# An attention kernel whose ring for x keeps six batches instead of eight

## The chip, the cores and the metric

One core of a Trainium2 chip. The metric is the device time of one execution in microseconds (us); lower is better. "A" and "B" are the two halves of the problem, and a "unit" is one head of one batch (512 units, 256 in A and then 256 in B). The kernel works the units off in order.

## The reference, cut to what matters

Two equal attention blocks with their own inputs, whose outputs are put side by side (16 batches, 144 rows of width 448, 16 heads of 256, 512 cached keys, all bfloat16):

```
q = (x @ wq).reshape(B, Sq, H, Dh).transpose(0, 2, 1, 3)
scores = einsum("bhqd,bhkd->bhqk", q, k_cache) * Dh ** -0.5
o = einsum("bhqk,bhkd->bhqd", softmax(scores), v_cache)
out = o.transpose(0, 2, 1, 3).reshape(B, Sq, H * Dh) @ wo
```

## The kernel before

A scheduler of the kernel's own writes one instruction list per engine, in the order of a loop over units, and puts in only the waits that are needed. Step `i` of the loop issues the Q product of unit `i+3`, the scores of unit `i+2`, and the product with V, the softmax sum and some output projection of unit `i`. All loads are issued by one queue (SP) in one fixed order.

First, x arrives transposed in groups of four batches, in a ring of eight:

```
LQ, LS, LT = 3, 2, 4
KW, KR = 16, 32
NV, NXG = 9, 2
XB = 4
# ... cut ...
xt_sb = sb("xt_sb", [128, 4, NXG * XB * SQ], BF16)
# ... cut ...
def t_load_x(XG):
    pr, j = divmod(XG, Bn // XB)
    sl = XG % NXG
    c0 = sl * XB * SQ
    x = xs[pr][j * XB:(j + 1) * XB].rearrange("b q d -> (b q) d")
    def e(q):
        q.dma_start_transpose(xt_sb[:, 0:3, c0:c0 + XB * SQ], x[:, 0:384]).then_inc(sems["xt%d" % sl], 16)
        return q.dma_start_transpose(xt_sb[:, 3, c0:c0 + XB * SQ], x[:, 320:448]).then_inc(sems["xt%d" % sl], 16)
    # ... cut ...
```

Second, Q is computed for two neighbouring batches of one head at once (8 matmuls of 288 columns) where the two lie side by side in the ring; where they don't, one batch at a time (8 matmuls of 144 columns each). For odd heads that happens at batches 7 and 8:

```
def q_pair(U):          # how many batches the Q product at unit U computes
    b, h = unit(U)[1:]
    # ... cut: single products in the first four batches of A ...
    if h % 2 == 0:
        return 2 if b % 2 == 0 else 0
    j = b % (NXG * XB)
    return 1 if j in (0, NXG * XB - 1) else (2 if j % 2 else 0)
```

Third, K arrives transposed, one load of 4.19 MB for 16 units ("K step" n serves units 16n to 16n+15), with V in between, and where A gives way to B the query weights (q0 to q3) and the output weights (o0 to o7) of B have to be loaded too. The order there is fixed by hand:

```
MID = ("k16 v127 v128 q0 v129 v130 q1 v131 q2 q3 v132 k17 v133 v134 v135 v136 v137 o0 o1 v138 o2 v139 o3 v140 o4 v141 "
       "o5 v142 o6 o7 k18")
# ... cut: each x load goes into the order just ahead of the first K load that may come after it
elif fn is t_load_k:
    lo = KW * (args[0] + 1) - KR - LS               # earliest step: the K slot is free
elif fn is t_load_x and args[0] >= NXG:
    lo = (args[0] - NXG + 1) * XB * H - LQ          # earliest step: the x slot is free
elif fn is t_load_wq and args[0]:
    lo = NU - H + 4 * args[1] + 4 - LQ              # earliest step: A is done with these weights
```

## Time and profile before

| | |
|---|---|
| time, median of 4 | 1066.06 us (1065.64 to 1066.65) |
| the profiled execution | 1063.18 us, span 1061.4 us |
| PE (TensorE) busy | 98% |
| share of PE in the chain that ended last | 97% |
| PE idle for loads, in all | 12.7 us |

The page of the profile gives the busy time of each engine, the queues by which DMA packets were moved, and the chain of work that ended last (the share of the span that lies with each engine or line). PE is TensorE, PEld its weight loads, DVE VectorE, ACT ScalarE, POOL GpSimd; SPq is the queue of loads, and L1018 is line 1018 of the kernel.

```profile
PE 1043.1 (98%) x12736; PEld 895.5 (84%) x12736; DVE 670.9 (63%) x2063; ACT 706.4 (67%) x2133; POOL 625.6 (59%) x1030
...
q8 instruction: 102, 1.67, 0.6%
...
PE 97%; DMA 2%; SPq 1%; DVE 0%; issue 0%; ACT 0%; DVEq 0%
PE s_ps L1052 24%; PE ot_ps L1097 24%; PE qp_ps L1018 24%; PE op_ps L1196 20%; PE ot_ps L1109 3%; DMA v_sb<-in_A_k_cache_dram 1%; PE s_ps L972 1%; PE qp_ps L972 1%; PE qp_ps L1196 1%; DMA v_sb<-in_B_v_cache_dram 1%; SPq L922 0%; SPq L923 0%; DVE ost_sb L1217 0%; SPq L902 0%; DVE run_sb L1154 0%
```

PE is busy nearly throughout and is nearly the whole chain. "q8 instruction" is, as its count will show, the queue that fetches PE's program: 102 packets of 16 KB.

The view of waits lists what PE waited for (total us, number of waits, longest):

```profile
PE s_ps L972 <- DMA v_sb<-in_A_k_cache_dram: 6.1, 4, 4.7
PE qp_ps L1018 <- DMA xt_sb<-in_A_x_dram: 3.6, 1, 3.6
PE ot_ps L1097 <- DMA v_sb<-in_B_v_cache_dram: 3.0, 1, 3.0
```

(The first three K steps are an exception to the transposed loads: their K comes in plain tiles of 512 KB into the buffers of V, hence `v_sb<-in_A_k_cache`, and PE transposes them.) So PE waits for K, x and V only 12.7 us in all. The first load of x is at fault for 3.6 us near the start. The queue's own timeline (start, duration, what) shows why: the two transposes of the first x load hold the queue 3.57 and 1.87 us, and the second K tile cannot be issued before 7.97 us:

```profile
2.44 3.57 SPq L922 DMA_TRANSPOSE xt_sb<-in_A_x_dram  x1
6.05 1.87 SPq L923 DMA_TRANSPOSE xt_sb<-in_A_x_dram  x1
7.97 0.59 SPq L953 DMA_DIRECT2D v_sb<-in_A_k_cache_dram  x1
```

In the chain of waits, start and duration of a Q product of two batches (0.98 us) and of one batch (0.50 us):

```profile
555.67 0.98 PE qp_ps L1018 x8
558.09 0.50 PE qp_ps L1018 x8
```

Two single products cost 1.00 us and a pair 0.98: PE is paid by columns, not by instructions.

PE's timeline between the problems (start, duration, what, in brackets the idle time before and its cause):

```profile
566.88 1.14 PE L1097 MATMUL ot_ps<-pt_sb,v_sb 128*128 128x144 bf16 x8 [3.05 <-DMA v_sb<-in_B_v_cache_dram]
...
568.68 2.13 PE L1018 MATMUL qp_ps<-xt_sb,wq_sb 128*128 128x288 bf16 x8
...
573.04 0.66 PE L1018 MATMUL qp_ps<-xt_sb,wq_sb 128*128 128x144 bf16 x8
```

V comes 3.05 us late, and for some 6 us after it matmuls run at half speed: the 8 matmuls of the pair at 568.68 take 2.13 us, where 1.14 is usual in this view.

### The profile page before, as it was taken

The numbers are of one execution on the slowest core, as the hardware profiler recorded it, in microseconds if no ns is written. First come the engines' busy times: TensorE is split into PE (matmuls) and PEld (weight loads), VectorE is DVE, ScalarE is ACT, GpSimd is POOL, SyncE is SP. The second block draws the span as 40 slices with busy tenths as digits, with TensorE's granted clock in tenths as the row PEclk, the third lists the DMA queues.
The fourth block names the chain that finished last, engine by engine and source line by source line (L and its number), as shares of the span: only waits on it lengthen the run. The fifth ranks groups of instructions, "written<-read, shape, count | busy, mean of one in ns | idle before, by whom it ended". The sixth has DMA issues, their size and how long they took to land.

```text
span 1061.4 us, 32383 instructions
## 1 busy us (share of the span) xinstructions
PE 1043.1 (98%) x12736; PEld 895.5 (84%) x12736; DVE 670.9 (63%) x2063; ACT 706.4 (67%) x2133; POOL 625.6 (59%) x1030
## 2 busy tenths in 40 slices
PE   6999999999999999999998999999999999999997
PEld 6999888888888888888887888888888888888885
DVE  4776666666666666666665666666666666666664
ACT  4887656667756666666855666676775666667674
POOL 3554555656656566666754656566665555666663
PEclk9999999999999999999998999999999999999999
DMA  9999999999999999999999999999999999999950
GB/s 304 379 350 285 295 293 254 274 297 273 292 276 298 208 280 267 290 292 298 262 287 352 265 274 290 291 290 301 264 263 265 304 285 289 289 290 279 239 187 13
DMA packets 588801, 294.15 MB, mean 277 GB/s; under 512 B 500576, under 2 KB 513376, under 8 KB 588640
## 3 DMA queue, kind: packets, MB, share of 16 engines
q1 hardware_dynamic: 588640, 291.99, 109.1%
q8 instruction: 102, 1.67, 0.6%
q14 instruction: 59, 0.48, 0.2%
HBM read 161.48 MB, written 4.13 MB: 156 GB/s over the span
## 4 chain that ended last, share of the span: by engine, by line
PE 97%; DMA 2%; SPq 1%; DVE 0%; issue 0%; ACT 0%; DVEq 0%
PE s_ps L1052 24%; PE ot_ps L1097 24%; PE qp_ps L1018 24%; PE op_ps L1196 20%; PE ot_ps L1109 3%; DMA v_sb<-in_A_k_cache_dram 1%; PE s_ps L972 1%; PE qp_ps L972 1%; PE qp_ps L1196 1%; DMA v_sb<-in_B_v_cache_dram 1%; SPq L922 0%; SPq L923 0%; DVE ost_sb L1217 0%; SPq L902 0%; DVE run_sb L1154 0%
## 5 line engine op out<-in xcount | busy, mean ns | idle before, releaser
L1072 POOL TENSOR_TENSOR pp_sb<-pt_sb 128x288 f32<-128x288 bf16 x512 | 374.0, 731 | 345.7 <-ACT pt_sb L1062 323.5
L1062 ACT ACTIVATE pt_sb<-s_ps 128x288 bf16<-128x288 f32 x1024 | 364.4, 408 | 268.5 <-PE s_ps L1052 268.0
L1154 DVE TENSOR_REDUCE run_sb<-ot_ps 1x1 bf16<-1x144 f32 x1024 | 262.3, 293 | 324.0 <-ACT rinv_sb L1120 324.0
L1097 PE MATMUL ot_ps<-pt_sb,v_sb 128*128 128x144 bf16 x4096 | 340.7, 226 | 3.0 <-DMA v_sb<-in_B_v_cache_dram 3.0
L1052 PE MATMUL s_ps<-qt_sb,kt_sb 128*128 128x144 bf16 x4096 | 340.8, 226 | 0.0
L1052 PEld LDWEIGHTS s_ps<-qt_sb,kt_sb 128*128 128x128 bf16 x4096 | 288.2, 98 | 43.5 <-DVE qt_sb L1032 0.2
L1018 PE MATMUL qp_ps<-xt_sb,wq_sb 128*128 128x288 bf16 (+1 forms) x2496 | 305.3, 266 | 3.6 <-DMA xt_sb<-in_A_x_dram 3.6
L1076 POOL TENSOR_TENSOR ps_sb<-pp_sb 128x144 bf16<-128x144 f32 x512 | 250.8, 490 | 76.2 <-PE ot_ps L1109 3.1
L1018 PEld LDWEIGHTS qp_ps<-xt_sb,wq_sb 128*128 128x128 bf16 x2496 | 218.8, 98 | 79.0 <-issue 4.4
L1196 PE MATMUL op_ps<-wo_sb,ring 128*128 128x448 bf16 x1120 | 285.0, 353 | 0.4 <-DVE ring L1140 0.4
L1097 PEld LDWEIGHTS ot_ps<-pt_sb,v_sb 128*128 128x128 bf16 x4096 | 274.6, 98 | 3.7 <-DMA v_sb<-in_B_v_cache_dram 3.2
L1140 DVE TENSOR_TENSOR ring<-ot_ps,rinv_sb 128x288 bf16<-128x288 f32 (+2 forms) x640 | 231.0, 375 | 0.0
L1120 ACT ACTIVATE rinv_sb<-ot_ps 128x144 f32<-128x144 f32 x512 | 150.1, 293 | 51.0 <-PE ot_ps L1109 8.0
L1032 DVE CAST qt_sb<-qp_ps 128x576 bf16<-128x576 f32 x200 | 151.1, 755 | 41.7 <-PE qp_ps L1018 37.6
L1125 ACT ACTIVATE rinv_sb<-rinv_sb 128x144 f32<-128x144 f32 x512 | 165.4, 323 | 16.1
L1109 PE MATMUL ot_ps<-ps_sb,ones 128*128 128x144 bf16 x512 | 115.9, 226 | 0.0
L1196 PEld LDWEIGHTS op_ps<-wo_sb,ring 128*128 128x128 bf16 x1120 | 94.0, 98 | 21.8 <-DVE ring L1140 0.8
L1031 DVE CAST qt_sb<-qp_ps 128x288 bf16<-128x288 f32 x112 | 49.2, 439 | 9.4 <-PE qp_ps L1018 8.8
L1109 PEld LDWEIGHTS ot_ps<-ps_sb,ones 128*128 128x128 bf16 x512 | 50.2, 98 | 0.0
L980 ACT ACTIVATE kt_sb<-qp_ps 128x512 bf16<-128x512 bf16 x48 | 28.9, 603 | 8.5 <-PE qp_ps L972 8.5
L972 PE MATMUL s_ps<-qt_sb,v_sb 128*128 128x128 bf16 x192 | 19.4, 226 | 6.2 <-DMA v_sb<-in_A_k_cache_dram 6.1
L980 DVE COPY kt_sb<-s_ps 128x512 bf16<-128x512 bf16 x48 | 19.5, 405 | 6.3 <-PE s_ps L972 6.2
(21 smaller groups left out, 85.1 us busy)
## 6 DMA issues: line engine op xcount, KB each, us to landing
v_sb<-in_A_v_cache_dram SPq DMA_DIRECT2D x128, 512.0 KB, 6.9
v_sb<-in_B_v_cache_dram SPq DMA_DIRECT2D x128, 512.0 KB, 7.1
v_sb<-in_A_k_cache_dram SPq DMA_DIRECT2D x24, 512.0 KB, 9.3
out_dram<-ost_sb SPq DMA_DIRECT2D x36, 112.0 KB, 6.1
wo_sb<-in_A_wo_dram SPq DMA_DIRECT2D x8, 448.0 KB, 8.5
wo_sb<-in_B_wo_dram SPq DMA_DIRECT2D x8, 448.0 KB, 8.9
wq_sb<-in_A_wq_dram SPq DMA_DIRECT2D x4, 768.0 KB, 9.2
wq_sb<-in_B_wq_dram SPq DMA_DIRECT2D x4, 768.0 KB, 10.1
```

The costliest lines, as they stand in the source:

```text
L1018: ins = t.matmul(acc, lhsT=wq_sb[:, kc, c0:c0 + 128], rhs=xt_sb[:, kc, xo:xo + n * SQ], start=(kc == 0), stop=(kc == 3))
L1032: return v.tensor_copy(qt_sb[:, a:b + 1:b - a, :, :], qp_ps[:, :, 0:2 * SQ].rearrange("p e (u q) -> p u e q", u=2))
L1052: ins = t.matmul(s_ps[bank][:, (c % 2) * SQ:(c % 2 + 1) * SQ], lhsT=kt_sb[:, 2 * c + dc, ko:ko + 128], rhs=qt_sb[:, qsl, dc, :], start=(dc ...
L1062: return a.activation(pt_sb[:, psl, 2 * k:2 * k + 2, :].rearrange("p b q -> p (b q)"), s_ps[bank][:, 0:2 * SQ], AF.Exp, scale=DH ** -0.5)
L1072: return g.tensor_tensor(pp_sb[:, :, :], pt_sb[:, psl, 0:2, :], pt_sb[:, psl, 2:4, :], op=ALU.add)
L1076: return g.tensor_tensor(ps_sb[:, sl, :], pp_sb[:, 0, :], pp_sb[:, 1, :], op=ALU.add)
L1097: ins = t.matmul(ot_ps[ob][:, dc * SQ:(dc + 1) * SQ], lhsT=v_sb[:, vsl, j, c * DH + dc * 128:c * DH + (dc + 1) * 128], rhs=pt_sb[:, sl, c, ...
L1109: return t.matmul(ot_ps[ob][:, 2 * SQ:3 * SQ], lhsT=ones[:, :], rhs=ps_sb[:, sl, :], start=True, stop=True)
L1125: return a.activation(rinv_sb[:, sl, :], ln, AF.Exp, scale=-1.0)
L1140: ins = v.tensor_tensor(ring[:, 2 * h:2 * h + 2, r0:r0 + q1 - q0], ot_ps[ob][:, 0:2 * SQ].rearrange("p (c q) -> p c q", c=2)[:, :, q0:q1], ...
L1154: return v.tensor_reduce(run_sb[0:1, k, j:j + 1], ot_ps[ob][0:1, 2 * SQ:3 * SQ], axis=AX.X, op=op)
L1196: ins = t.matmul(acc[0:m, 0:D], lhsT=ring[:, c, col0:col0 + m], rhs=wo_sb[:, c, :], start=(c == first), stop=(c == last))
```

## The change

Its intent: keep x for six batches only, which frees 2.3 KB per partition of SBUF (not used yet), load the first two batches alone so that work starts sooner, and let a pair of batches wrap round the ring, so that the odd heads of batches 7 and 8 are paired as well. The diff, cut to its core:

```diff
-    NV, NXG = 9, 2
+    NV, NX = 9, 6
-    XB = 4
+    X_GROUPS = ((0, 2), (2, 6), (6, 10), (10, 14), (14, 18), (18, 20), (20, 24), (24, 28), (28, 32))
@@ t_load_x
+            cuts = [g for g in range(g0, g1) if g == g0 or g % NX == 0 or g % Bn == 0] + [g1]
+                for a, b in zip(cuts, cuts[1:]):   # one pair of transposes for each piece
@@ q_pair
-            j = b % (NXG * XB)
-            return 1 if j in (0, NXG * XB - 1) else (2 if j % 2 else 0)
+            return 1 if b in (0, Bn - 1) else (2 if b % 2 else 0)
@@ t_q
-                                       rhs=xt_sb[:, kc, xo:xo + n * SQ], start=(kc == 0), stop=(kc == 3))
+                                       rhs=xt_sb[:, kc, xo:xe + 1:max(xe - xo, 1), :], start=(kc == 0), stop=(kc == 3))
@@ earliest step of an x load
+            last = X_GROUPS[XG][1] - NX
+            return last * H - LQ if last > 0 else s_min
```

One consequence is not in the diff: the order of loads changes. Before, x is loaded ahead of K steps 5, 9, 13, 19, 21 and 25. After, it is loaded ahead of 5, 9, 13, 15, 19, 23 and 27. The load ahead of step 15 (batches 2 and 3 of B) is new there.

## The prediction

> What bounds the kernel. TensorE: the page's busy table gives PE 1043.1 of 1061.4 us (98%), clock 0.996; the chain of waits is PE for 97%. The DMA engines are nine tenths busy in nearly every slice, but in the waits view PE idles little for them: 6.1 us for K rows (s_ps L972), 3.6 us for x (qp_ps L1018), 3.0 us for V (ot_ps L1097). In time order: the first Q product waits until 9.96 us for x, the second K row tile is used at 12.39 us, waits of 0.3 and 0.2 us follow at 25.7 and 34.0 us; then PE has no gap until 563.8 us, where V is 3.05 us late behind problem B's second K load (26.85 us in the queue), and for 6 us after it matmuls run at half speed (8 pair matmuls in 1.92 us, not 0.98).
>
> What the change does.
> 1. Q. Odd heads of batches 7 and 8 of both problems join: 32 single products become 16 pairs, 128 matmuls (of 12736) fewer. But PE is paid by columns: in the chain a single product takes 0.50 us, a pair 0.98, so each pairing saves 0.02 us, 0.3 us in all. The Trainium skill ("TensorE: Matmul & The Clock Gate", Back-to-back issue gap) gives N/2.4 + 2.5 ns per warm matmul; 0.50/8 = 62 ns and 0.98/8 = 122 ns agree. DVE trades 32 casts of 439 ns for 16 of 755 ns, off the chain (63% busy).
> 2. Start. The first x load has two batches instead of four. Its two transposes held the queue 3.57 + 1.87 us, so the second K tile was issued only at 7.97 us; this is on the chain (SPq L922, L923, then DMA into v_sb). Halved, I estimate 2.5 us off. Afterwards the DMA engines are saturated (387 GB/s) and PE touches their limit at 25.7 and 34.0 us; both shift together, so the gain should stay.
> 3. Later x loads. 24 transposes instead of 16, same bytes. The second load is now needed at unit 29 (about 78 us); it left the queue at 64.7. Later ones are due 16 or 17 units (32 us) before use, just ahead of a K load. An x plus a K load held the queue 22 to 28 us (K alone 16 to 27). The last two move ahead of the K loads issued at 736 and 863 us; K and V have, I estimate, 3 to 5 us to spare there, as at existing x loads, which stalled nothing.
> 4. The SBUF freed is not used.
>
> Sum: 1066.05 - 2.5 - 0.3, plus 0.3 for the chance of a new stall: 1063.5 us. The gap at 564 us should stay. A new stall would cost its length plus some 3 us of half clock.
>
> Range 1059.5 to 1068. Faster by over 2%: 1%; within 2%: 97%; slower by over 2%: 2%.
>
> What would show it: 12608 PE instructions, yet the Q lines' time on the chain only 0.3 us lower; first Q product at about 7.5 us, second K tile used at about 9.8 us, all later work earlier by that; PE idle on x about 1 us; the gap near 561 us still 3 us.
>
> What would make it wrong: a half-size transpose costs the queue as much as a whole one (gain under 1 us); an x load late at a wrap, or pushing K or V late: PE waiting on xt_sb, kt_sb or v_sb with half-clock work after it (+3 to +8 us each); the 564 us gap closing or growing with DMA timing.

## The result, and the profile after

The changed kernel took 1066.12 us (median of 4, 1065.60 to 1067.24), the kernel before 1066.06. The ratio is 1.0002, 95% interval 0.9984 to 1.0019: the same. (A ratio here is the mean time of one kernel's fast executions over that of the other's of the same rounds, so it is not quite the ratio of the medians.) The time lies in the predicted range, but the gain that was forecast, 2.5 us, is not there.

The page after:

```profile
PE 1044.1 (98%) x12608; PEld 892.0 (84%) x12608; DVE 671.0 (63%) x2047; ACT 706.0 (66%) x2133; POOL 625.6 (59%) x1030
...
q8 instruction: 101, 1.65, 0.6%
...
PE 96%; DMA 3%; SPq 0%; DVE 0%; issue 0%; ACT 0%; DVEq 0%
PE s_ps L1063 24%; PE ot_ps L1108 24%; PE qp_ps L1029 23%; PE op_ps L1207 20%; PE ot_ps L1120 3%; DMA v_sb<-in_A_k_cache_dram 1%; PE s_ps L977 1%; PE qp_ps L977 1%; DMA v_sb<-in_B_v_cache_dram 1%; DMA wq_sb<-in_B_wq_dram 1%; PE qp_ps L1207 1%; DMA xt_sb<-in_A_x_dram 0%; SPq L925 0%; DVE ost_sb L1228 0%; SPq L902 0%
```

PE has 128 matmuls and 128 weight loads fewer, and its program needs one packet of 16 KB fewer (101 instead of 102).

At the start the queue is free 2.8 us earlier, as forecast: the two transposes take 1.43 and 1.23 us, and the second K tile is issued at 5.19 us instead of 7.97:

```profile
2.44 1.43 SPq L925 DMA_TRANSPOSE xt_sb<-in_A_x_dram  x1
3.91 1.23 SPq L926 DMA_TRANSPOSE xt_sb<-in_A_x_dram  x1
5.19 0.58 SPq L958 DMA_DIRECT2D v_sb<-in_A_k_cache_dram  x1
```

The waits of PE are others, though:

```profile
PE s_ps L977 <- DMA v_sb<-in_A_k_cache_dram: 5.8, 3, 4.9
PE qp_ps L1029 <- DMA wq_sb<-in_B_wq_dram: 3.6, 1, 3.6
PE qp_ps L1029 <- DMA xt_sb<-in_A_x_dram: 2.4, 1, 2.4
PE s_ps L1063 <- DMA kt_sb<-in_B_k_cache_dram: 1.9, 1, 1.9
PE ot_ps L1108 <- DMA v_sb<-in_B_v_cache_dram: 1.1, 2, 0.6
```

The wait for x is 1.2 us shorter and the one for V in B 1.9 us, but two are new: 3.6 us for the query weights of B and 1.9 us for K of B. The first of them in PE's timeline:

```profile
534.02 2.08 PE L1029 MATMUL qp_ps<-xt_sb,wq_sb 128*128 128x288 bf16 x8 [3.58 <-DMA wq_sb<-in_B_wq_dram]
535.90 1.17 PE L1063 MATMUL s_ps<-qt_sb,kt_sb 128*128 128x144 bf16 x8
...
539.47 0.66 PE L1063 MATMUL s_ps<-qt_sb,kt_sb 128*128 128x144 bf16 x8
```

The idle time of 3.58 us is followed by half-speed work (2.08 us for the pair at 534.02).

To see where time goes, I read from the timelines the start of one instruction that each unit has exactly once (the logarithm on ScalarE, 512 of them) and took the difference after minus before, unit by unit:

| unit | after minus before, us | what lies between |
|---|---|---|
| 0 | -2.18 | the start |
| 32 to 96 | -1.75 | nothing changes |
| 124 | +2.10 | Q of batch 8 is computed early, with batch 7 |
| 140 to 224 | -1.90 | it is given back in batch 8: net -0.16 |
| 256 | +4.36 | wait for the query weights of B, and half-speed work |
| 267 | -0.97 | before has its V wait here, after only 0.6 us |
| 288 | +3.52 | wait for K step 18, and half-speed work |
| 320 to 352 | +3.38 | nothing changes |
| 416 to 480 | +3.22 | batches 7 and 8 of B: again -0.16 |

So the start gives 1.75 us and each set of pairs 0.16 us, and the lead of 1.90 us is there up to unit 240. It is lost between units 240 and 288. (The 3.2 us at the end is more than the timed executions show: the profiled execution of the kernel before, 1063.18 us, was a fast one.)

The queue's timeline shows what comes ahead of the late weights. Before:

```profile
475.91 16.30 SPq L932 DMA_TRANSPOSE kt_sb<-in_A_k_cache_dram  x1
...
505.82 16.97 SPq L932 DMA_TRANSPOSE kt_sb<-in_B_k_cache_dram  x1
...
523.97 0.47 SPq L900 DMA_DIRECT2D wq_sb<-in_B_wq_dram  x1
```

After:

```profile
471.09 1.22 SPq L925 DMA_TRANSPOSE xt_sb<-in_B_x_dram  x1
...
474.01 19.36 SPq L937 DMA_TRANSPOSE kt_sb<-in_A_k_cache_dram  x1
...
503.92 19.62 SPq L937 DMA_TRANSPOSE kt_sb<-in_B_k_cache_dram  x1
...
524.73 0.47 SPq L900 DMA_DIRECT2D wq_sb<-in_B_wq_dram  x1
```

K step 16 (the transpose at 505.82 before, 503.92 after) holds the queue for 19.62 us instead of 16.97, and the query weights, issued behind it, come that much later in relation to the work. K step 15 (at 474.01) holds it for 19.36 us; before it was 16.30 (at 475.91).

### The profile page after: what moved, and what is told of

It reads as the page before. It is cut to its first block, busy times and chain, and to the rows that moved or that the text cites. A ratio compares the mean times of both kernels' runs of the same rounds, so it can differ in the third digit from the quotient of the medians.

```text
span 1064.6 us, 32119 instructions
## 1 busy us (share of the span) xinstructions
PE 1044.1 (98%) x12608; PEld 892.0 (84%) x12608; DVE 671.0 (63%) x2047; ACT 706.0 (66%) x2133; POOL 625.6 (59%) x1030
## 4 chain that ended last, share of the span: by engine, by line
PE 96%; DMA 3%; SPq 0%; DVE 0%; issue 0%; ACT 0%; DVEq 0%
PE s_ps L1063 24%; PE ot_ps L1108 24%; PE qp_ps L1029 23%; PE op_ps L1207 20%; PE ot_ps L1120 3%; DMA v_sb<-in_A_k_cache_dram 1%; PE s_ps L977 1%; PE qp_ps L977 1%; DMA v_sb<-in_B_v_cache_dram 1%; DMA wq_sb<-in_B_wq_dram 1%; PE qp_ps L1207 1%; DMA xt_sb<-in_A_x_dram 0%; SPq L925 0%; DVE ost_sb L1228 0%; SPq L902 0%
## 5 line engine op out<-in xcount | busy, mean ns | idle before, releaser
L1029 PEld LDWEIGHTS qp_ps<-xt_sb,wq_sb 128*128 128x128 bf16 x2368 | 213.3, 99 | 81.7 <-issue 7.5
L1043 DVE CAST qt_sb<-qp_ps 128x576 bf16<-128x576 f32 x216 | 163.3, 756 | 49.5 <-PE qp_ps L1029 45.4
L1042 DVE CAST qt_sb<-qp_ps 128x288 bf16<-128x288 f32 x80 | 35.2, 440 | 5.7 <-PE qp_ps L1029 5.1
```

The lines of the kernel that those rows point to most:

```text
L1029: ins = t.matmul(acc, lhsT=wq_sb[:, kc, c0:c0 + 128], rhs=xt_sb[:, kc, xo:xe + 1:max(xe - xo, 1), :], start=(kc == 0), stop=(kc == 3))
L1043: return v.tensor_copy(qt_sb[:, a:b + 1:b - a, :, :], qp_ps[:, :, 0:2 * SQ].rearrange("p e (u q) -> p u e q", u=2))
```

## The experiments

Twelve runs (ten new kernels and the two old ones again) were made in three sessions, on three chips, each of which ran the kernel before as well (its medians: 1066.05, 1067.37 and 1065.74 us; in the second session it scattered from 1065.7 to 1071.2, so that ratios of that session, experiments 5 to 8, come out low). The labels of theories in the quoted expectations: A, the two-batch x load ahead of K step 15 makes the weights late by its place in the queue; B, the waits come and go by chance; C, that load makes them late by its DMA work; D, the wrapped pairs make them late; E, the fetches of PE's own program do, F, ring and x load alone suffice. In the table, "units 240 to 256" has 29.0 us where PE does not wait, "K16 held" is how long K step 16 held the queue, and each trace is of one execution only.

| kernel | median us (n) | ratio to before, 95% interval | K16 held | units 240 to 256 | units 240 to 288 |
|---|---|---|---|---|---|
| before (first profile) | 1066.06 (4) | | 16.97 | 29.0 | 101.0 |
| after (first profile) | 1066.12 (4) | 1.0002 (0.9984 to 1.0019) | 19.62 | 35.3 | 106.5 |
| 1 before, again | 1065.71 (5) | 0.9994 (0.998 to 1.0007) | 16.17 | 29.0 | 103.5 |
| 2 short start only | 1064.15 (5) | 0.9985 (0.9971 to 0.9999) | 16.03 | 29.0 | 104.1 |
| 3 wrapped pairs only | 1065.96 (5) | 0.9996 (0.9983 to 1.001) | 18.34 | 32.9 | 104.3 |
| 4 after, x load moved | 1066.11 (5) | 0.9996 (0.9983 to 1.001) | 21.69 | 36.3 | 107.9 |
| 5 late x load only | 1066.08 (6) | 0.998 (0.996 to 0.9999) | 16.36 | 29.0 | 103.9 |
| 6 short start and pairs | 1063.48 (6) | 0.9963 (0.9941 to 0.9985) | 17.85 | 30.3 | 102.3 |
| 7 after, again | 1067.56 (6) | 0.9995 (0.9974 to 1.0016) | 21.46 | 37.4 | 108.9 |
| 8 after, output weights later | 1070.81 (6) | 1.0029 (1.001 to 1.0049) | 19.95 | 34.1 | 100.7 |
| 9 before, two batches unpaired | 1066.16 (5) | 1.0009 (0.9995 to 1.0023) | 17.48 | 30.0 | 102.1 |
| 10 after, two batches unpaired | 1063.95 (5) | 0.9979 (0.9966 to 0.9993) | 18.03 | 31.0 | 104.3 |
| 11 after, query weights first | 1067.73 (5) | 1.002 (1.0006 to 1.0034) | 20.73 | 30.0 | 106.6 |
| 12 short start, pairs, weights first | 1066.78 (5) | 1.0007 (0.9993 to 1.002) | 20.72 | 29.8 | 108.3 |

### 1. The kernel before, again

No edit.

> The kernel before, unchanged, as a second profile of the same program. In the first profile it had one stall between the problems (V at 563.8 us, 3.05 us, then half clock) and its profiled execution took 1063.2 us, while its timed executions took 1065.6 to 1066.7. Theory A (the change really costs time between the problems: the two-batch x load ahead of the last K load of problem A makes the first weights of problem B late): this profile again has no wait for the B weights, and only the V stall. Theory B (the stalls between the problems come and go by DMA timing in both kernels, and the first profile was a lucky one): this profile shows other stalls there than the first, a wait for the B weights among them, and 2 to 4 us more.

Measured: 1065.71 us, the same. The waits between the problems:

```profile
PE ot_ps L1097 <- DMA v_sb<-in_B_v_cache_dram: 3.1, 2, 1.9
PE s_ps L1052 <- DMA kt_sb<-in_B_k_cache_dram: 2.5, 1, 2.5
```

There is no wait for the query weights, as theory A expected, but the V wait is smaller than in the first profile (two waits, 1.9 us at most, instead of 3.05) and K step 18 is late by 2.5 us, which the first profile did not show. So both theories are partly right: the waits for V and for K step 18 vary from one execution to the next in the kernel before (this is the scatter of a few us), but the wait for the query weights is not among them.

### 2. The short start alone

```diff
-    NV, NX = 9, 6
+    NV, NX = 9, 8
+    X_GROUPS = ((0, 2), (2, 8), (8, 12), (12, 16), (16, 20), (20, 24), (24, 28), (28, 32))
-            return 1 if b in (0, Bn - 1) else (2 if b % 2 else 0)
+            return 1 if b % 8 in (0, 7) else (2 if b % 2 else 0)
```

(the edits are against the changed kernel; the second group is loaded as two pieces)

> Ring of eight batches and Q pairs as before; only the first x load is cut to two batches and the second carries six. If the gain at the start is what the unit times of the two profiles show, every unit up to about 250 ends 1.75 us earlier than before (the first unit 2.2 us). Theory A: no new wait between the problems, so the time is 1064.3 us, ratio 0.998. Theory B: the stalls between the problems vary, the time is anything from 1062 to 1067 with the same 1.75 us lead up to unit 250.

Measured: 1064.15 us, ratio 0.9985. Unit 32 is 1.92 us ahead of the first profile of before, and stays so up to unit 256, without a wait for the query weights. The gain of the start reaches the end of the kernel.

### 3. The wrapped pairs alone

```diff
-    NV, NX = 9, 6
+    NV, NX = 9, 8
+    X_GROUPS = ((0, 4), (4, 8), (8, 12), (12, 16), (16, 20), (20, 24), (24, 28), (28, 32))
```

> Ring of eight, loads of four batches at their old places, but the odd heads of batches 7 and 8 are joined in pairs that wrap round the ring. 12608 PE instructions. Both theories: units before 110 unchanged; inside batch 7 units run up to about 4 us behind and get it back in batch 8, net lead of 0.16 us per problem, 0.3 us in all; the time is that of before within 0.3 us apart from the variable stalls (Theory A: no new stalls, 1065.7; Theory B: 1063 to 1067).

Measured: 1065.96 us, ratio 0.9996. Each problem gains 0.16 us at its batches 7 and 8, as expected. What was not expected by theory A: K step 16 holds the queue 18.34 us, and units 240 to 256 take 3.8 us longer (an idle time of 2.0 us at unit 253 and half-speed work). The profile names no cause for this idle time ("issue"); the product is the first that needs the new query weights:

```profile
534.83 1.54 PE L1029 MATMUL qp_ps<-xt_sb,wq_sb 128*128 128x288 bf16 x7 [2.04 <-issue]
```

There is no late x load here. Theory A cannot explain it.

### 4. The changed kernel with its late x load moved

```diff
+        dma_plan.remove((t_load_x, (5,)))
+        at = dma_plan.index((t_load_k, (15,)))
+        at = [k for k in range(at, len(dma_plan)) if dma_plan[k][0] is t_load_v][2] + 1
+        dma_plan.insert(at, (t_load_x, (5,)))
```

> The changed kernel with its two-batch x load of problem B moved from ahead of the last K load of problem A to behind it and three V loads, where the queue waits for V buffers anyway. Theory A: the wait for the B weights near 530 us (3.6 us and half clock after it, 6 us in all) goes, and with it the K wait near 611 us may remain; 1060 to 1064 us. Theory B: the wait for the B weights is there or not with no tie to this, and the median stays at 1066 within 1 us.

Measured: 1066.11 us, ratio 0.9996, and a wait of 4.6 us for the query weights:

```profile
PE qp_ps L1029 <- DMA wq_sb<-in_B_wq_dram: 4.6, 1, 4.6
```

Theory A falls: the place of that load ahead of K step 15 is not the cause. The run does not clear the load's DMA work, though: the load now stands among the V loads just ahead of K step 16, whose first packet came 5.6 us after its issue (1.3 us in the kernel before, 2.7 in the changed kernel).

### 5. The late x load alone

```diff
-    NV, NX = 9, 6
+    NV, NX = 9, 8
+    X_GROUPS = ((0, 4), (4, 8), (8, 12), (12, 16), (16, 18), (18, 20), (20, 24), (24, 28), (28, 32))
+    # (16, 18) ahead of K step 13, (18, 20) ahead of K step 15; pairs as before
```

> Ring of eight, old start, old Q pairs; the only change is that batches 2 and 3 of problem B, which the kernel before loads with batches 0 and 1 ahead of the 13th K step, are loaded by themselves ahead of the last K load of problem A (step 15), as the changed kernel does. Theory C (that late x load is the cost: it adds DMA work to the stretch in which K, the B weights and V fill the queue without a pause): the K load at unit 236 holds the queue 19 us or more instead of 16 to 17, a wait for the B weights appears at unit 253, and the time is 1067.5 to 1068.5, ratio 1.0015 to 1.0025. Theory D (the wrapped Q pairs bring it): 1066.0, ratio 1.000, no wait for the B weights.

Measured: 1066.08 us, ratio 0.998, K step 16 held 16.36 us, no wait for the query weights: theory C as it stood is wrong, and theory D's figures come out. But the experiment is weaker than I thought when I made it: it moves two batches from step 13 to step 15, while the changed kernel loads four at step 13 and two more at step 15. It shows that a load at that place costs nothing by itself; it doesn't show that two batches more are free.

### 6. Short start and wrapped pairs, ring of eight

```diff
-    NV, NX = 9, 6
+    NV, NX = 9, 8
+    X_GROUPS = ((0, 2), (2, 8), (8, 12), (12, 16), (16, 20), (20, 24), (24, 28), (28, 32))
```

> Ring of eight with the short first x load and with the wrapped Q pairs, and x loads of four batches at their old places, so without the late two-batch load. Theory C: both gains stay, 1066.05 - 1.9 - 0.2 = 1063.9, ratio 0.998, K load at unit 236 holds the queue 16 to 18 us. Theory D: 1066, ratio 1.000, wait for the B weights at unit 253.

Measured: 1063.48 us, the lowest median (executions from 1061.3 to 1066.3). (Its ratio of 0.9963 flatters it, because the kernel before scattered upwards in that session.) K step 16 held the queue 17.85 us, and units 240 to 256 took 1.3 us longer than without waits. Both gains stay, as theory C said; the pairs still cost a small wait, as theory D said, but not their whole gain.

### 7. The changed kernel, again

No edit.

> The changed kernel unchanged, as a second profile. If its stalls are a property of the program, the wait for the B weights at unit 253 (3 to 5 us) and the K wait at unit 286 (about 2 us) are there again and the K load at unit 236 holds the queue over 18 us; if they are luck, another set. Time 1066.1 within 0.5.

Measured: 1067.56 us, ratio 0.9995. The waits are there again, so they belong to the program:

```profile
PE qp_ps L1029 <- DMA wq_sb<-in_B_wq_dram: 5.4, 1, 5.4
PE s_ps L1063 <- DMA kt_sb<-in_B_k_cache_dram: 2.3, 1, 2.3
```

### 8. Part of the output weights later

```diff
-           "... k17 v133 v134 v135 v136 v137 o0 o1 v138 o2 v139 o3 v140 o4 v141 o5 v142 o6 o7 k18"
+           "... k17 v133 v134 v135 v136 v137 o0 v138 o1 v139 o2 v140 v141 v142 k18 v143 o3 o4 v144 o5 v145 o6 o7"
-    OP_DELAY, OP_START, OP_START_B = 2, 28, 20
+    OP_DELAY, OP_START, OP_START_B = 2, 28, 28
```

> The changed kernel with part of the output weights of problem B (five of eight loads) moved behind K step 18 in the queue and their first use put off by 8 units. If the queue is what limits PE from unit 253 to 288 (theories C and D alike), K step 18 starts about 6 us earlier and the K wait at unit 286 goes (about 2 us and its half clock): 1061.5 to 1064, with the waits at units 253 and 266 as before. If the wait at unit 286 has another cause, or the output weights then come late, 1066 or more.

Measured: 1070.81 us, ratio 1.0029, a miss. Units 240 to 288 took only 100.7 us, but the output projection that was put off has to be done afterwards, and K came 3.1 us late at a later step: units 288 to 480 took 392.0 us, where every other kernel took 382.0 to 382.3. Waits and work were only moved.

### What the traces say of K steps 15 and 16

The packets of 256 bytes in the traces are those of the transposes. Laid out over time, they show what makes a K load long. The DMA view of a window gives the rate in 40 equal slices. For the kernel before, 506 to 526 us, in slices of 0.5 us:

```profile
GB/s 414 57 111 149 159 264 286 285 291 284 188 111 289 291 288 291 291 290 291 312 142 1 9 144 290 289 291 289 291 290 289 290 290 290 291 291 378 53 238 393
...
q8 instruction: 2, 0.03, 0.7%
```

K step 16 runs at 290 GB/s from the sixth slice on, and then its rate falls to 1 and 9 GB/s for two slices. At that place the trace has one packet of 16 KB on the queue that fetches PE's program, which took 1.2 us. Such a packet comes about every 250 matmuls and weight loads (25472 of them, 102 packets). (The Trainium skill, "Runtime: NRT & Kernel Launch", Instruction fetch mechanics, says that programs are refilled in blocks of 16 KiB, 256 instructions, on a DMA queue of the sequencer's own, at a cost that is mostly hidden. The count agrees: 128 matmuls and 128 weight loads fewer are one packet fewer, 101 instead of 102. The cost is hidden from PE, but not from the transposes.) The changed kernel, 504 to 528 us, in slices of 0.6 us:

```profile
GB/s 396 386 382 389 342 166 71 151 309 83 7 131 290 291 290 291 290 291 290 291 290 291 290 291 314 157 5 90 289 291 289 291 289 300 145 269 300 399 338 280
```

Here there are two such holes, at slices 10 to 12 and 26 to 28. The load also begins later: V loads at nearly 390 GB/s still fill the first 3 us, where it was one slice of 0.5 us before. (Both windows begin 0.1 to 0.2 us after the K load is issued.) Over all 14 traces, K loads with one fetch inside them took 17.3 us from first to last packet (191 of them), those with two 18.9 us (125). (A fetch counts as inside from 2 us after the first to 2 us before the last packet; K loads mixed with an x load are left out. A long load has more room for two fetches, so this alone would not prove a cause.) But the holes keep to the fetches: in 545 of the 547 fetches inside a K load (those mixed with x loads counted too), the rate from 0.6 to 1.5 us after the fetch began was under 60 GB/s; its median was 6 GB/s, against 290 GB/s in the 1.5 us before the fetch. The holes themselves, read off the slices, cost 1.2 to 1.5 us each.

That gives a theory which the diff does not suggest. Up to K steps 15 and 16, the change takes away 64 matmuls and 64 weight loads, so 128 instructions: just half the period of the fetches. In the kernels with the old pairs, one fetch falls inside K step 16 (4.1 us after unit 240 in the first profile of before) and one at its end (12.6 us), where it does no harm. In kernels with wrapped pairs and the old order of loads they fall at -1.1 to +1.0 and at +9 us, both inside (in experiment 4 only the second, since the load itself begins at -0.3 us). Experiments 9 and 10 test it with one small edit that puts 128 instructions back.

### 9. The kernel before with two batches of A unpaired

```diff
             j = b % (NXG * XB)
+            if U < NU and b in (9, 10):
+                return 1
             return 1 if j in (0, NXG * XB - 1) else (2 if j % 2 else 0)
```

(the added lines stand ahead of the line with j; the order is without effect)

> The kernel before, with the odd heads of batches 9 and 10 of problem A taken out of their pairs: 128 more instructions on PE (64 matmuls, 64 weight loads) before batch 11, at a cost of 0.16 us. Theory E (the program's own instruction fetches, 16 KB on the DMA rings every 256 PE instructions, stop a K transpose for about 1.1 us each; 128 instructions more or less shift them by half a period, so that two instead of one fall inside K steps 15 and 16): fetches inside K step 16 near -1 and +9 us from unit 240 as in the kernels with wrapped pairs, the K load at unit 236 holds the queue 18 us or more (16.0 to 17.0 before), its last packet 13.5 to 14 us after unit 240 (11.8 to 12.6 before), and a wait for the B weights of 1 us or more at unit 253; time 1066 to 1067.5. Theory D (the wrapped pairs themselves): as before, no such wait, 1066.2.

Measured: the fetches fell at -0.9 and +9.0 us, as theory E said. The rate shows both holes (506 to 526 us, slices of 0.5 us):

```profile
GB/s 315 139 182 152 289 290 291 290 322 255 2 9 138 291 289 290 290 290 291 289 291 289 290 291 290 291 289 290 318 180 4 10 228 290 291 289 326 70 213 352
```

K step 16 held the queue 17.48 us (16.0 to 17.0 with the old pairs) and its last packet came 13.1 us after unit 240 (11.8 to 12.6), both a little less than expected; PE then had to wait 0.8 us at unit 253, where the kernel before did not in either profile:

```profile
532.86 1.14 PE L1020 MATMUL qp_ps<-xt_sb,wq_sb 128*128 128x288 bf16 x8 [0.83 <-DVE run_sb L1156]
```

(The profile names a DVE instruction as the cause; this is the one matmul that needs the new query weights, and the same instruction waits for them in the changed kernel.) The time, 1066.16 us, ratio 1.0009 (0.9995 to 1.0023), lies between 0.5 us less and 2.5 us more than that of the kernel before, which leaves its own effect on the time undecided. Direction and place are as theory E said, the size is at its lower end. Theory D falls: there is no wrapped pair in this kernel.

### 10. The changed kernel with the same batches unpaired

```diff
+            if U < NU and b in (9, 10):
+                return 1
             return 1 if b in (0, Bn - 1) else (2 if b % 2 else 0)
```

> The changed kernel with the same pairs of batches 9 and 10 of problem A taken apart, so that the PE instruction count up to the change of problems is that of the kernel before again. Theory E: fetches fall as before (one inside K step 16, near +4), the K load at unit 236 holds the queue 16 to 17.5 us, ends 12 to 13 us after unit 240, no wait for the B weights or one under 1 us, though ring and x loads are those of the changed kernel; time 1064.2, about 2 us under the kernel before. Theory F (the late two-batch x load together with the ring of six is enough): K load at unit 236 19 us or more, wait of 3 us or more for the B weights, 1066.

Measured: 1063.95 us, ratio 0.9979 (0.9966 to 0.9993). Making 8 pair products into 16 single ones makes the changed kernel 2 us faster. Its five executions (1062.5 to 1064.7) do not overlap with the ten of the changed kernel (1065.5 to 1069.4), which ran in other sessions; the intervals of the ratios to the kernel before do overlap a little. The fetches are back at -5.9, +4.0 and +13.8 us; one hole is left inside, at slices 18 to 20, but V loads still fill the first 2.4 us (504 to 528 us, slices of 0.6 us, from 0.2 us before the issue of the K load):

```profile
GB/s 393 379 386 329 161 46 23 169 289 291 289 291 289 291 289 291 313 157 4 48 292 288 292 288 292 288 292 288 292 288 292 288 301 150 249 317 358 229 239 413
```

The wait for the query weights is 1.8 us, where the changed kernel had 3.6 and 5.4, and after 1.8 us the clock did not drop (V comes 3.2 us late afterwards, within the scatter of that wait):

```profile
PE ot_ps L1110 <- DMA v_sb<-in_B_v_cache_dram: 5.1, 2, 3.2
PE qp_ps L1031 <- DMA wq_sb<-in_B_wq_dram: 1.8, 1, 1.8
```

But 1.8 us is not the zero of the kernel before, and K step 16 held the queue 18.03 us, more than theory E allowed. The last packet came 14.1 us after unit 240 with the fetches as in the kernel before, 13.1 to 14.0 with shifted fetches and the ring of eight, and 15.8 to 17.4 with both (the changed kernel twice, experiments 4 and 8). So there are two parts, and the ring of six brings the second.

### 11. The first query weights of B ahead of K step 16

```diff
-    MID = ("k16 v127 v128 q0 v129 v130 q1 v131 q2 q3 v132 k17 ...
+    MID = ("q0 k16 v127 v128 q1 v129 v130 q2 v131 q3 v132 k17 ...
```

> The changed kernel with the first quarter of problem B's query weights moved ahead of K step 16 in the queue. If the wait for the B weights at unit 253 is what takes the gain away: it is gone in every run, and the time is 1063 to 1064.5. If the whole stretch from unit 236 to 288 is set by the sum of the loads in the queue, the waits only move to V at unit 266 and K at unit 286, and the time is 1065.5 to 1067.

Measured: 1067.73 us, ratio 1.002. The wait for the query weights is gone, and one of 6.5 us for V has come in its place:

```profile
PE ot_ps L1108 <- DMA v_sb<-in_B_v_cache_dram: 7.1, 2, 6.5
PE s_ps L1063 <- DMA kt_sb<-in_B_k_cache_dram: 1.3, 1, 1.3
```

In time this is the second of the two outcomes, and somewhat worse than it. But the edit did more than change an order: the query weights may be loaded only when A is done with the old ones, so the queue stood still in front of them, and K step 16, now behind them, was issued 0.1 us before unit 240 instead of 5.9 us before it:

```profile
508.41 0.37 SPq L900 DMA_DIRECT2D wq_sb<-in_B_wq_dram  x1
...
509.38 20.73 SPq L937 DMA_TRANSPOSE kt_sb<-in_B_k_cache_dram  x1
```

So this run shows that holding K step 16 back by 5.8 us costs more than the earlier weights save; it does not tell whether the loads between units 236 and 288 would leave room if only the order changed.

### 12. The same with short start, pairs and ring of eight

```diff
-    MID = ("k16 v127 v128 q0 ...     (in the kernel of experiment 6)
+    MID = ("q0 k16 v127 v128 q1 ...
```

> Ring of eight, short first x load, wrapped pairs, and the first quarter of the B query weights ahead of K step 16: the candidate for the best kernel. 1062 to 1063.5, no wait for the B weights; if the sum of the loads sets the stretch, 1063.5 to 1064.5 as without the move.

Measured: 1066.78 us, 3 us slower than expected of the better case, with 8.0 us of waiting for V at one place. K step 16 was held back by 5.8 us here too. The order by hand of the kernel before is better than mine.

## Why the prediction was right or wrong

The time was right (1066.1 us, predicted 1063.5, range 1059.5 to 1068), but the gain in it was not: 2.5 us were forecast and none came. That the time lies in the range is luck as far as the mechanism goes: the range was wide enough to hold "no gain" as well. Point by point:

- **PE bounds the kernel.** Right.
- **Pairs save 0.3 us in all.** Right: 0.16 us per problem in every trace with wrapped pairs.
- **The start gains 2.5 us, and it stays because PE and DMA shift together.** Right in size: the mean start of unit 32 is 85.2 us in the nine traces with the short first load and 87.5 us in the five without, 2.35 us. Right also that it can stay: experiment 2 kept it. Some details were off: the first Q product came at 9.02 us (7.5 forecast) and PE idled 2.4 us on x (1 forecast).
- **"plus 0.3 for the chance of a new stall."** This is the step that failed. A new stall was there in both traces of the changed kernel and in its two relatives (experiments 4 and 8): 3.3 to 5.4 us of waiting for the query weights at unit 253, with half-clock work 5.1 to 8.3 us on units 240 to 256. Part of it comes back, since PE then arrives later at the waits for V and K that the kernel before has as well: units 240 to 288 took 106.5 and 108.9 us against 101.0 and 103.5 (and 103.9 and 104.1 in experiments 5 and 2, which have no such wait either). The term was 0.3 us and should have been about 2.5 us, the size of the gain, as the timed executions have it. The prediction's own list of what would make it wrong named waits on xt_sb, kt_sb and v_sb; the largest was on wq_sb, which it had not thought of. Its price for a stall was about right: 3.6 us of waiting cost 6.3 us on units 240 to 256.
- **Where I looked for stalls.** I costed the slack at the two last x loads, ahead of the K loads at 736 and 863 us. No stall came there. I had the new load ahead of K step 15 in front of me in the order of loads and did not cost it, and I did not ask how much room there is behind K step 16: before, the query weights arrive just in time.
- **"The gap at 564 us should stay."** Wrong, and without meaning: it was 3.05 us in one execution of the kernel before and two waits of at most 1.9 us in another.

What made the query weights late has two parts. The first is shown by experiments 9 and 10, which change the instruction count and, long before K step 16, the Q products of batches 9 and 10, and nothing else: 128 PE instructions fewer shift the program's own fetches by half a period, so that two of them stop K step 16 where one did. Putting 128 instructions back in the changed kernel brings 2 us, most of the lost gain. The second part, some 1.4 to 2.3 us at the end of K step 16 that are left in experiment 10, comes with the ring of six and its x loads.

Neither part costs time by itself. The kernels with the short first load make a square (medians in us; the sessions differ, but experiments 6 and 7 share one; experiment 2 alone has the old pairs, which are worth 0.3 us, and each ring has its own x loads):

| | fetches as before | fetches shifted |
|---|---|---|
| ring of eight | 1064.15 (experiment 2) | 1063.48 (experiment 6) |
| ring of six | 1063.95 (experiment 10) | 1066.12 and 1067.56 (the changed kernel, first run and experiment 7) |

With the long first load, too, shifted fetches alone left the time where it was (1065.96 and 1066.16 us in experiments 3 and 9). It takes both to make the query weights so late that the gain is lost.

As to how the ring of six brings its part: I argue that it is the DMA work of two more batches of x between K steps 13 and 15 (six instead of four), which leaves V loads on their way when K step 16 starts: 2.4 and 3 us of them in experiment 10 and the changed kernel, 0.5 us in the kernel before. (With the order of loads by hand kept, K step 16's first packet came 1.3 us after its issue in every trace with the ring of eight, and 1.6 to 5.6 us after it in every trace with the ring of six.) No run separates it: experiment 5 moved a load and did not add one. It stays open.

## What to carry to other kernels

A gain at the start of this program was kept only where the later stretch in which the queue of loads has no slack did not get worse; look for these stretches first (here the change from one problem to the next), and cost what the change adds ahead of them, even two small loads. Removing instructions from an engine shifts where its program is fetched, and where long DMA transposes have little slack, that phase can decide whether a small gain is kept: here it cost about 2 us with the ring of six, and nothing that could be told from scatter with the ring of eight. Before explaining a small loss, restore the instruction count by some other means and measure. If a ring of eight can stay, the short first load with the wrapped pairs (1063.5 us) has a median some 2.5 us under both kernels; with a ring of six, taking two batches apart again (1063.95 us) does nearly as well.

## What the Trainium skill lacked or had wrong

- "Runtime: NRT & Kernel Launch", Instruction fetch mechanics, calls the fetch of a 16 KiB block mostly hidden. The runs show that such a fetch, one packet of about 1 us, stops a running DMA transpose of K altogether: two slices of 0.5 us at 10 GB/s or less between slices at 290, 1.2 to 1.5 us lost each time (the rate fell in 545 of the 547 fetches well inside a K load). No page has this.
- "DMA: Bandwidth & Descriptors", Latency and other measured facts, gives 261 GB/s as the effective rate of a DMA transpose with a non-contiguous middle dimension, and about 350 to 400 GB/s for the contiguous case. Here the K transposes, whose source is one contiguous block, ran at 290 GB/s in undisturbed slices and at 256 GB/s over a whole load with one fetch in it (4.19 MB in 16.4 us, K step 16 of experiment 1): under the page's figure for the contiguous case. Why is open; no run changed the layout.
- "TensorE: Matmul & The Clock Gate", Part 1, gives about 3.4 us of idle time before the clock is halved. Here half-speed work followed a single gap of 2.0 us (experiment 3) and of 3.05 us, but not gaps of 1.8 us (experiment 10), 2.85 us (experiment 9) and 3.13 us (experiment 2); the page does say that its window is free-running.
